# Blocks 4 to 11 in pairs: 512 tokens per up product, four down accumulators, six pooled PSUM banks, and an order written out

## The chip, the cores and the metric

The kernel runs on one core of a Trainium2 chip, in one launch. The metric is the device time of one execution in microseconds. The core's engines run at the same time and meet at semaphores: TensorE (PE) multiplies and writes to PSUM, VectorE (DVE) and ScalarE (ACT) read PSUM and compute element by element, GpSimd (POOL) computes element by element in SBUF, SyncE (SP) issues DMA.

## What is computed

A gated linear attention over 4 batches, 8 heads, 768 tokens and 40 values per head gives a state C and a normaliser n per head; its output y feeds a two-layer block. Everything is float32.

```python
for t in range(S):                       # attention, S = 768
    m_new = np.maximum(f_gate[:, :, t] + m, i_gate[:, :, t])
    f_stab = np.exp(f_gate[:, :, t] + m - m_new); i_stab = np.exp(i_gate[:, :, t] - m_new)
    C = f_stab * C + i_stab * (v_t outer k_t);  n = f_stab * n + i_stab * k_t
    y[:, :, t] = sigmoid(o_gate) * (C @ q_t) / max(|n . q_t|, 1)
x = y as (3072 tokens, 320)
h = x @ w_in                             # 320 -> 2048
sp = np.maximum(h, 0.0) + np.log1p(np.exp(-np.abs(h)))
out = (h * erf(sp)) @ w_out              # 2048 -> 320
```

The weights arrive as float64 and are decoded on the chip into a high and a low fp32r half (wh, wl for w_in; woh, wol for w_out).

## The kernel before

**Attention steps.** A chunk is 128 tokens; six chunks of four batches make 24 steps s. Step s loads q and k (`load`), k, v and the output gate (`loadv`), from chunk 1 on also rows of decays (`dq`) and of gate sums (`bq`, which reads cum_dr, written earlier by SP). POOL adds to the latter (`add`), ACT takes exp (`ex`), POOL masks it (`sel`). PE computes scores (`S`) and then outputs and new state (`ph`), DVE multiplies, adds and divides around them (`w`, `qa`, `sa`, `sk`, `yg`), ACT takes tanh of the gate (`th`), PE transposes the result (`tr`), and ACT and DVE split it into a high and a low half (`xh`, `xl`). From step 10 on, tr, S and ph of three neighbouring steps are one unit X on PE.

**Blocks and phases.** Two steps (256 tokens, T) make one of 12 blocks. A block passes through two phases, each with half of the 2048 hidden values, so there are 24 phases f. A phase has two groups of four 128-wide slices. In a group PE makes two up parts (`up`, L1023), each of two slices by eight products of 256 columns (high and low halves over three pieces of the 320 inputs) into one PSUM bank; `hb` copies each part out (DVE L1034 or ACT L1032); `sp` (L1046) and `er` (L1050) are softplus and erf on ACT, which loads a table at each switch; `mu` (DVE L1058) multiplies; `gh` (ACT L1064) and `gl` (DVE L1069) split it; then PE makes two down parts (`dn`, L1104, L1105, L1107), one for each of the block's two 128-token accumulators po0 and po1, each of 12 products of 320 columns. After the last group `o` (L1124) copies an accumulator out and `st` (L1131) stores it. Phases 0 and 1 use whole float32 weights (L1100). Until PE has work, it makes dummy products on a warm-up tile (`fill`, L445).

**Memory.** The eight PSUM banks are four for attention (`pa`), two for up parts (`h`), and po0 and po1. In SBUF a pool of 26 buffers of 4 KB per partition (`big`) holds loads, weights in work, and hb, e, gh, gl, xh and xl.

**Order.** A planner (class Plan) orders the parts by due times, costs per part, and tables of corrections, and issues them. On each engine the instructions run in that order, and an instruction at the head of its queue waits for its semaphores with all others of that engine behind it.

Of the kernel before, what the change touches and what calls it, by code (L numbers as in the profile page):

```python
# [9 lines left out]
F32 = mybir.dt.float32  # L10
# [19 lines left out]
NB = 2  # L30
# [10 lines left out]
class Buf:  # L41
    def __init__(self, tag):
        self.tag, self.users, self.left = tag, [], 0
        self.tags = ('big', tag) if tag in CAPS else (tag,)
# [6 lines left out]
class Plan:  # L51


    LAG = dict(PE=0.25, DVE=0.05, ACT=0.14, POOL=0.06, SP=0.0)
    RATE = 370.0
    AWAY, LANDING = 1.0, 1.2
    BEGIN = dict(SP=0.8, DVE=0.8, ACT=0.8, POOL=0.3, PE=0.8, dma=2.4)
    TABLE = 1.3
    FETCH = 5.8
    WINDOW, SINCE = 3.413, 1.3  # L60
    ENTER = {(3, 'D'): 0.1, (3, 'U'): 0.17, (1, 'D'): 0.22, (1, 'U'): 0.29, (2, 'D'): 0.22, (2, 'U'): 0.29, (1, 3): 0.12,
             (2, 3): 0.12, (1, 2): 0.1, (2, 1): 0.1, (3, 1): 0.09, (3, 2): 0.09, ('D', 1): 0.09, ('U', 1): 0.09,
             ('D', 2): 0.09, ('U', 2): 0.09}

    def __init__(self, slots):
        self.parts, self.slots, self.filler = [], dict(slots), None
        self.reset()

    def add(self, engine, cost, n=0, *, fn, after=(), new=(), use=(), target=None, kb=0.0, table=None, mode=0, order=(), lock=False):
        p = Part()  # L70
        p.engine, p.cost, p.fn, p.kb, p.table, p.mode, p.size = engine, cost, fn, kb, table, mode, n
        p.after = [x for x in after if x is not None]
        p.order = [x for x in order if x is not None]
        p.new, p.target, p.n = list(new), target, len(self.parts)
        for b in (*new, *use):
            b.users.append(p)
        p.held = [*new, *use]
        p.into, p.leaves, p.lock = None, mode, lock or engine == 'POOL'
        self.parts.append(p)
        return p  # L80

    def merge(self, name, members):
        p = self.add(members[0].engine, 0.0, fn=lambda: [m.fn() for m in members], mode=members[0].mode)
        p.name, p.leaves, p.size = name, members[-1].mode, sum(m.size for m in members)
        p.cost = sum(m.cost for m in members) + sum(self.ENTER.get((x.mode, y.mode), 0.0) for x, y in zip(members, members[1:]))
        p.after, p.order = ([x for m in members for x in getattr(m, of)] for of in ('after', 'order'))
        p.new = [b for m in members for b in m.new]
        p.held = list(dict.fromkeys(b for m in members for b in m.held))
        p.target = min((m.target for m in members if m.target is not None), default=None)
        for m in members:  # L90
            m.into = p
        for b in p.held:
            b.users = [x for x in b.users if x.into is not p] + [p]
        return p

    def tick(self, t, cost):

        while cost > 1e-9:
            k = max(0, int((t - self.SINCE) / self.WINDOW))
            while len(self.warm) <= k:  # L100
                busy = self.busy[len(self.warm) - 1] / self.WINDOW
                self.warm.append(busy > (0.65 if self.warm[-1] else 0.9))
                self.busy.append(0.0)
            pace = 1.0 if self.warm[k] else 2.0
            d = min(self.SINCE + (k + 1) * self.WINDOW - t + 1e-9, cost * pace)
            self.busy[k] += d
            t, cost = t + d, cost - d / pace
        return t

    def stream(self, t, cost, n):  # L110

        if not n:
            return self.tick(t, cost)
        each, end = cost / n, self.count + n
        while self.count < end:
            k = self.count // 256 + 1
            to = 256 * k - 48
            to = min(end, to if self.count < to else 256 * k)
            t, self.count = self.tick(t, (to - self.count) * each), to
            if to == 256 * k - 48:  # L120
                self.there[k + 1] = max(t, self.there.get(k, 0.0)) + self.FETCH
            elif to == 256 * k:
                t = max(t, self.there.get(k, 0.0))
        return t

    def reset(self):
        self.count, self.there, self.warm, self.busy = 68, {}, [True], [0.0]

    def lag(self, p):
        return self.AWAY + self.LANDING + p.kb / self.RATE if p.engine == 'SP' else self.LAG[p.engine]  # L130

    def issue(self):
        parts = self.parts = [p for p in self.parts if p.into is None]
        for i, p in enumerate(parts):
            p.n = i
            for of in ('after', 'order'):
                found = dict.fromkeys(x.into or x for x in getattr(p, of))
                found.pop(p, None)
                setattr(p, of, list(found))
# [1109 lines left out]
```

## Time and profile before

| | us |
|---|---|
| median of 3 runs | 476.99 (476.94 to 480.74) |
| span of the profiled execution | 474.6 |
| PE busy | 465.5 |
| PE weight loads busy | 433.4 |
| DVE busy | 336.2 |
| ACT busy | 330.7 |
| POOL busy | 117.9 |

The page counts an engine as busy while at least one instruction is in it. PE's products overlap, so the price of one in a stream is the distance between two starts, which the timeline shows. An engine's idle time costs nothing by itself; what matters is which wait ends last in a stage.

### The profile page before, as it was taken

The numbers are of one execution on the slowest core, as the hardware profiler recorded it, in microseconds if no ns is written. First come the engines' busy times: TensorE is split into PE (matmuls) and PEld (weight loads), VectorE is DVE, ScalarE is ACT, GpSimd is POOL, SyncE is SP. The second block draws the span as 40 slices with busy tenths as digits, with TensorE's granted clock in tenths as the row PEclk, the third lists the DMA queues.
The fourth block names the chain that finished last, engine by engine and source line by source line (L and its number), as shares of the span: only waits on it lengthen the run. The fifth ranks groups of instructions, "written<-read, shape, count | busy, mean of one in ns | idle before, by whom it ended". The sixth has DMA issues, their size and how long they took to land.

```text
span 474.6 us, 13831 instructions
## 1 busy us (share of the span) xinstructions
PE 465.5 (98%) x6091; PEld 433.4 (91%) x6095; DVE 336.2 (71%) x565; ACT 330.7 (70%) x385; POOL 117.9 (25%) x99
## 2 busy tenths in 40 slices
PE   9997999999999999999999999999999999999996
PEld 3567687999999999999999999999999999999996
DVE  4688799964688988897688498587487576466451
ACT  3574997499937998858655779458379556579670
POOL 2222147100912304043021454123453121010000
PEclk9998999999999999999999999999999999999999
DMA  7999525801174426045414405515313000000000
GB/s 260 381 298 308 141 93 177 301 1 55 47 227 134 106 88 185 1 152 161 136 43 135 135 17 155 143 35 156 122 35 120 19 17 15 1 17 13 1 28 28
DMA packets 28879, 53.25 MB, mean 112 GB/s; under 512 B 3060, under 2 KB 17844, under 8 KB 28820
## 3 DMA queue, kind: packets, MB, share of 16 engines
q1 hardware_dynamic: 28820, 52.38, 35.4%
q8 instruction: 47, 0.77, 0.7%
q14 instruction: 12, 0.10, 0.1%
HBM read 48.27 MB, written 4.10 MB: 110 GB/s over the span
## 4 chain that ended last, share of the span: by engine, by line
PE 88%; DMA 10%; SPq 1%; DVE 0%; POOL 0%; issue 0%; ACT 0%; POOLq 0%
PE h L1023 37%; PE po L1104 12%; PE po L1107 11%; PE po L1105 11%; PE pa L700 5%; DMA kvo<-in_kvo_dram 4%; PE po L1100 4%; PE pa L734 3%; DMA raw<-in_w_out_dram 3%; PE pa L738 3%; DMA raw<-in_w_in_dram 2%; PE pa L796 1%; PE pa L743 1%; DMA dq<-dec_dr 1%; PE po L445 0%; POOL wol L989 0%
## 5 line engine op out<-in xcount | busy, mean ns | idle before, releaser
L1023 PE MATMUL h<-xl,wh 128*128 128x256 f32 x576 | 158.1, 285 | 2.2 <-issue 1.9
L1023 PE MATMUL h<-xh,wh 128*128 128x256 f32 x576 | 158.7, 286 | 0.6 <-ACT xh L809 0.6
L1023 PEld LDWEIGHTS h<-xh,wh 128*128 128x128 f32 x576 | 111.1, 193 | 1.4 <-ACT xh L809 0.8
L1023 PEld LDWEIGHTS h<-xl,wh 128*128 128x128 f32 x576 | 111.1, 193 | 0.8 <-DVE xl L827 0.4
L1023 PE MATMUL h<-xh,wl 128*128 128x256 f32 x384 | 109.3, 285 | 0.8 <-issue 0.8
L1104 PE MATMUL po<-woh,gh 128*128 128x320 f32 x352 | 106.9, 316 | 0.0
L1105 PE MATMUL po<-wol,gh 128*128 128x320 f32 x352 | 104.6, 309 | 0.0
L1034 DVE COPY hb<-h 128x512 f32<-128x512 f32 x84 | 58.0, 690 | 62.8 <-PE h L1023 61.5
L1023 PEld LDWEIGHTS h<-xh,wl 128*128 128x128 f32 x384 | 74.1, 193 | 3.0 <-issue 3.0
L1046 ACT ACTIVATE e<-hb 128x1024 f32<-128x1024 f32 x48 | 50.3, 1057 | 26.1 <-DVE hb L1034 25.8
L1104 PEld LDWEIGHTS po<-woh,gh 128*128 128x128 f32 x352 | 66.2, 188 | 1.4 <-issue 0.2
L1105 PEld LDWEIGHTS po<-wol,gh 128*128 128x128 f32 x352 | 66.3, 188 | 0.0
L1107 PE MATMUL po<-woh,gl 128*128 128x320 f32 x352 | 66.2, 309 | 0.0
L1069 DVE TENSOR_TENSOR gl<-hb,gh 128x1024 fp32r<-128x1024 f32 x44 | 56.7, 1298 | 8.3 <-ACT gh L1064 7.9
L1058 DVE TENSOR_TENSOR hb<-e,hb 128x1024 f32<-128x1024 f32 x44 | 56.2, 1282 | 9.0 <-ACT e L1050 8.9
L1064 ACT ACTIVATE gh<-hb 128x1024 fp32r<-128x1024 f32 x44 | 45.6, 1050 | 24.1 <-DVE hb L1058 21.3
L784 POOL TENSOR_TENSOR kvo<-kvo,den 128x320 f32<-128x320 f32 x18 | 21.6, 1202 | 147.3 <-DVE kvo L778 78.8
L1107 PEld LDWEIGHTS po<-woh,gl 128*128 128x128 f32 x352 | 55.2, 188 | 0.2 <-issue 0.2
L1050 ACT ACTIVATE e<-e 128x1024 f32<-128x1024 f32 x48 | 49.0, 1053 | 0.3
L641 POOL TENSOR_TENSOR dm<-dm,aT 128x1024 f32<-128x1024 f32 x18 | 38.9, 2166 | 39.9 <-DVE aT L545 18.5
L716 DVE TENSOR_TENSOR dm<-pa,dm 128x512 f32<-128x512 f32 x48 | 30.9, 684 | 17.9 <-PE pa L700 15.9
L1046 ACT ACT_TABLE_LOAD x30 | 38.5, 1283 | 0.8 <-DVE hb L1034 0.3
(119 smaller groups left out, 636.9 us busy)
## 6 DMA issues: line engine op xcount, KB each, us to landing
kvo<-in_kvo_dram SPq DMA_DIRECT2D x24, 484.0 KB
dm<-cum_dr SPq DMA_DIRECT2D x18, 512.0 KB
qk<-in_qk_dram SPq DMA_DIRECT2D x12, 512.0 KB
qk<-in_qk_dram SPq DMA_DIRECT2D x12, 416.0 KB
raw<-in_w_in_dram SPq DMA_DIRECT2D x8, 512.0 KB
out_dram<-o SPq DMA_DIRECT2D x24, 160.0 KB
raw<-in_w_out_dram SPq DMA_DIRECT2D x8, 320.0 KB
dq<-dec_dr SPq DMA_DIRECT2D x20, 128.0 KB
```

Of the source, the lines that this page charges most:

```text
L641: nc.gpsimd.tensor_tensor(v.dm, v.dm, G.aT[:, b].unsqueeze(2).to_broadcast([128, H, L]), op=ALU.add)
L716: nc.vector.tensor_tensor(v.w[:, j], v.ps[j], v.w[:, j], op=ALU.mult)
L1023: nc.tensor.matmul(V.h[i][:, n % 2 * T:(n % 2 + 1) * T], w, m, start=(q == 0), stop=(q == len(ops) - 1))
L1034: nc.vector.tensor_copy(V.hb[:, i * 512:(i + 1) * 512], V.h[i])
L1046: nc.scalar.activation(V.e, V.hb, AF.Softplus)
L1050: nc.scalar.activation(V.e, V.e, AF.Erf)
L1058: nc.vector.tensor_tensor(V.g if full else V.hb, V.e, V.hb, op=ALU.mult)
L1064: nc.scalar.activation(V.gh, V.hb, AF.Copy)
L1069: (nc.gpsimd if f in GL_POOL else nc.vector).tensor_tensor(V.gl, V.hb, V.gh.bitcast(F32), op=ALU.subtract)
L1104: nc.tensor.matmul(K.po[b], V.gh[:, ts], woh[:, w], start=start, stop=False)
L1105: nc.tensor.matmul(K.po[b], V.gh[:, ts], wol[:, w], start=False, stop=False)
L1107: nc.tensor.matmul(K.po[b], V.gl[:, ts], woh[:, w], start=False, stop=stop)
```

## The change

Blocks 0 to 3 keep their phases. Blocks 4 to 11 are taken in four pairs: a pair has four phases of two groups, and a group has two 128-wide slices of 512 tokens instead of four of 256. An up part is then one slice of eight products of 512 columns, which fill one bank. A pair needs all four steps of its chunk before its first up part, and it has four accumulators, po0 to po3; a down part is two accumulators of six products of 320 columns. The four attention banks, the two up banks, po2 and po3 come from one pool of six (`bank`). xh and xl of a chunk are one wider buffer each, from a pool `xx` of four (6 KB per partition); `big` has 20 buffers. The planner is gone: a list of 1,292 parts, written out, gives the order, found by a search over orders.

```diff
-SLOTS = dict(pa=4, h=2, po0=1, po1=1, big=26, vg=2, dq=2, ...)
+SLOTS = dict(bank=6, po0=1, po1=1, big=20, xx=4, vg=2, dq=2, ...)
+BANKS = dict(pa=4, h=2, po2=1, po3=1)
...
-ORDER = [(k, hh) for hh in range(2) for k in range(EARLY)] + [(k, hh) for k in range(EARLY, NK) for hh in range(2)]
+PAIRED = 4
+ORDER = [((k,), hh) for hh in range(2) for k in range(EARLY)] + [((k,), hh) for k in range(EARLY, PAIRED) for hh in range(2)]
+ORDER += [((k, k + 1), q) for k in range(PAIRED, NK, 2) for q in range(4)]
+SEQUENCE = """
+ident small gload0 select minus fill cst win01 +1 zeros mask +1 load0 +1 tail0 +2 scan0 ones +1 loadv1 sum0 +1
...
     def new(pool, shape, dtype, tag):
-        return pool.tile(shape, dtype, name=tag, bufs=SLOTS[tag])
+        kind = 'bank' if tag in BANKS else tag
+        return pool.tile(shape, dtype, name=tag, tag=kind, bufs=SLOTS[kind])
...
+        nb = NB * len(ks)
+        width, nj = nb * L, W // (nb * L)
...
+                mine = range(nj * p + i * nj // 2, nj * p + (i + 1) * nj // 2)
...
-                            nc.tensor.matmul(V.h[i][:, n % 2 * T:(n % 2 + 1) * T], w, m,
+                            nc.tensor.matmul(V.h[i][:, n * width:(n + 1) * width], w, m,
                                              start=(q == 0), stop=(q == len(ops) - 1))
...
-                        K.po[b] = new(ps, [128, 512], F32, f"po{b}")[:, 0:DM]
+                        K.po[half] = [new(ps, [128, 512], F32, f"po{b}")[:, 0:DM] for b in of]
...
-    parts = plan.issue()
     with tc.manual_schedule():
-        for p in parts:
-            p.fn()
+        plan.issue(SEQUENCE)
```

On PE, half of an up part of blocks 4 and later before (one of its two slices; h is the bank, xh and xl the halves of x, wh and wl those of w_in):

```order
L1023 MATMUL h_3558<-xh_2985,wh_78 128x256
L1023 MATMUL h_3558<-xl_2986,wh_78 128x256
L1023 MATMUL h_3558<-xh_2985,wl_79 128x256
L1023 MATMUL h_3558<-xh_2985,wh_78 128x256
L1023 MATMUL h_3558<-xl_2986,wh_78 128x256
```

and the start of a whole one after (the two xx are the halves of x, of four steps):

```order
L840 MATMUL h_3870<-xx_3191,wh_78 128x512
L840 MATMUL h_3870<-xx_3192,wh_78 128x512
L840 MATMUL h_3870<-xx_3191,wl_79 128x512
L840 MATMUL h_3870<-xx_3191,wh_78 128x512
L840 MATMUL h_3870<-xx_3192,wh_78 128x512
```

A product has twice the columns, and a part has 8 products instead of 16.

On SP, the first loads of the program before (gt gates, raw float64 weights, qk and kvo the inputs of a step):

```order
L427 DMA cst<-in_consts_dram 128x12
L495 DMA gt<-in_gates_dram 128x2x128
L891 DMA raw<-in_w_in_dram 128x1024
L578 DMA qk<-in_qk_dram 128x1024 x2
L589 DMA kvo<-in_kvo_dram 128x968 x2
L906 DMA raw<-in_w_in_dram 64x1024 x2
L578 DMA qk<-in_qk_dram 128x1024
L891 DMA raw<-in_w_in_dram 128x1024 x2
L578 DMA qk<-in_qk_dram 128x1024
```

and after:

```order
L304 DMA gt<-in_gates_dram 128x2x128
L235 DMA cst<-in_consts_dram 128x12
L703 DMA raw<-in_w_in_dram 128x1024
L387 DMA qk<-in_qk_dram 128x1024
L718 DMA raw<-in_w_in_dram 64x1024 x2
L398 DMA kvo<-in_kvo_dram 128x968
L703 DMA raw<-in_w_in_dram 128x1024
L398 DMA kvo<-in_kvo_dram 128x968
L387 DMA qk<-in_qk_dram 128x1024 x2
```

The two qk, two kvo, and the raw pieces of the first block stand first; the qk of steps 2 and 3 and a further piece of w_in, which stood among them, come later (load1 is the first of the last x2).

On SP, the loads of steps 12 to 14 before (the qk in the middle of the first four rows is that of step 13):

```order
L1131 DMA out_dram<-o 128x320
L581 DMA qk<-in_qk_dram 104x1024
L1131 DMA out_dram<-o 128x320
L637 DMA dm<-cum_dr 128x1024
L589 DMA kvo<-in_kvo_dram 128x968
L581 DMA qk<-in_qk_dram 104x1024
```

and after (the first qk is that of step 13, dm that of step 14, the last two qk those of steps 14 and 15):

```order
L951 DMA out_dram<-o 128x320
L410 DMA dq<-dec_dr 64x4x128
L410 DMA dq<-dec_dr 40x4x128
L951 DMA out_dram<-o 128x320
L390 DMA qk<-in_qk_dram 104x1024
L446 DMA dm<-cum_dr 128x1024
L390 DMA qk<-in_qk_dram 104x1024 x2
```

X13 is the first part on PE that reads the qk of step 13. Before, 18 parts of PE (X11, X12, eight up and eight down parts) stand between that load and X13 in the order of parts; after, two down parts do.

## Rows read from the trace of the kernel before

**Rows 1.** From the page, part 1: engines, busy us (share), instructions.

```profile
PE 465.5 (98%) x6091; PEld 433.4 (91%) x6095; DVE 336.2 (71%) x565; ACT 330.7 (70%) x385; POOL 117.9 (25%) x99
```

**Rows 2.** From the page, the chain that ended last: its shares of the span by line.

```profile
PE h L1023 37%; PE po L1104 12%; PE po L1107 11%; PE po L1105 11%; PE pa L700 5%; DMA kvo<-in_kvo_dram 4%; PE po L1100 4%; PE pa L734 3%; DMA raw<-in_w_out_dram 3%; PE pa L738 3%; DMA raw<-in_w_in_dram 2%; PE pa L796 1%; PE pa L743 1%; DMA dq<-dec_dr 1%; PE po L445 0%; POOL wol L989 0%
```

**Rows 3.** Busy us by stage: length, PE, PEld, DVE, ACT, POOL, clock, DMA, GB/s.

```profile
0.00:34.47 34.47, 32.97 (x469) 17.74 (x472) 22.34 (x59) 18.39 (x34) 7.59 (x16) 1.00 0.91 313
34.47:87.58 53.11, 49.28 (x638) 40.27 (x637) 46.04 (x91) 39.00 (x61) 20.01 (x16) 0.97 0.61 189
87.58:470.80 383.22, 383.13 (x4990) 375.38 (x4988) 267.83 (x417) 272.88 (x289) 90.28 (x68) 1.00 0.28 84
470.80:474.60 3.80, 0.16 (x2) 0.00 (x0) 0.00 (x0) 0.44 (x1) 0.00 (x0) 0.91 0.18 63
```

**Rows 4.** PE timeline: start us, us, instruction; and line L445's durations, ns.

```profile
421.36 0.28 PE L1023 MATMUL h<-xh,wh 128*128 128x256 f32 x1
...
423.28 0.31 PE L1104 MATMUL po<-woh,gh 128*128 128x320 f32 x1
...
425.04 0.28 PE L1023 MATMUL h<-xh,wh 128*128 128x256 f32 x1
...
19.34 2.56 PE L445 MATMUL po<-warm 128*128 128x512 bf16 x11 [0.16 <-issue]
...
L445 PE MATMUL po<-warm x61: 378/379/634, 1.1 to 49.6; 128*128 128x512 bf16 x61
```

**Rows 5.** From the page, costliest groups: busy us, mean ns, idle before it.

```profile
L1034 DVE COPY hb<-h 128x512 f32<-128x512 f32 x84 | 58.0, 690 | 62.8 <-PE h L1023 61.5
L1046 ACT ACTIVATE e<-hb 128x1024 f32<-128x1024 f32 x48 | 50.3, 1057 | 26.1 <-DVE hb L1034 25.8
L1069 DVE TENSOR_TENSOR gl<-hb,gh 128x1024 fp32r<-128x1024 f32 x44 | 56.7, 1298 | 8.3 <-ACT gh L1064 7.9
L1058 DVE TENSOR_TENSOR hb<-e,hb 128x1024 f32<-128x1024 f32 x44 | 56.2, 1282 | 9.0 <-ACT e L1050 8.9
L1064 ACT ACTIVATE gh<-hb 128x1024 fp32r<-128x1024 f32 x44 | 45.6, 1050 | 24.1 <-DVE hb L1058 21.3 <-PE h L1023 2.7
L1050 ACT ACTIVATE e<-e 128x1024 f32<-128x1024 f32 x48 | 49.0, 1053 | 0.3
L1046 ACT ACT_TABLE_LOAD x30 | 38.5, 1283 | 0.8 <-DVE hb L1034 0.3
```

**Rows 6.** PE's waits: us in total, times, the longest us.

```profile
PE h L1023 <- issue: 2.7, 2, 1.9
```

**Rows 7.** PE timeline around the longest of them, and the window after it.

```profile
41.08 0.28 PE L1023 MATMUL h<-xh,wh 128*128 128x256 f32 x1
43.26 0.28 PE L1023 MATMUL h<-xl,wh 128*128 128x256 f32 x1 [1.90 <-issue]
...
45.00:48.00 3.00, 3.00 (x19) 3.00 (x18) 2.08 (x7) 2.40 (x4) 0.00 (x0) 0.62 0.68 167
```

**Rows 8.** SP's issues of one load and of three, and the last window with bytes.

```profile
119.16 0.33 SPq L637 DMA_DIRECT2D dm<-cum_dr  x1
...
122.00:123.00 1.00, 1.00 (x11) 1.00 (x10) 0.64 (x2) 1.00 (x3) 1.00 (x1) 1.00 0.09 33
...
263.53 0.35 SPq L637 DMA_DIRECT2D dm<-cum_dr  x1
...
265.11 0.35 SPq L581 DMA_DIRECT2D qk<-in_qk_dram  x1
...
271.00:272.00 1.00, 1.00 (x15) 0.83 (x15) 0.83 (x2) 1.00 (x2) 0.00 (x0) 1.00 0.07 25
```

**Rows 9.** ACT's waits from 90 to 470 us: total, times, longest.

```profile
ACT kvo L657 <- DMA kvo<-in_kvo_dram: 7.7, 3, 5.8
```

**Rows 10.** Timeline at the end: the last down products, and the last copy.

```profile
470.21 0.75 PE L1107 MATMUL po<-woh,gl 128*128 128x320 f32 x4
471.00 0.44 ACT L1124 ACTIVATE o<-po 128x320 f32<-128x320 f32 x1 [1.32 <-PE po L1107]
```

More of the change, by code (lines that the diff above doesn't have):

```diff
@@ L51, with __init__ @@
 class Plan:
[L54 to L67, printed above, removed]
+    def __init__(self):
+        self.parts, self.filler = [], None
     def add(self, engine, cost, n=0, *, fn, after=(), new=(), use=(), target=None, kb=0.0, table=None, mode=0, order=(), lock=False):
         p = Part()
[L71 to L78, printed above, removed]
+        p.fn, p.order, p.into = fn, [], None
         self.parts.append(p)
@@ L82, in merge @@
     def merge(self, name, members):
[L83 to L87, printed above, removed]
@@ L88, in merge @@
-        p.held = list(dict.fromkeys(b for m in members for b in m.held))
-        p.target = min((m.target for m in members if m.target is not None), default=None)
+        p = self.add('PE', 0.0, fn=lambda: [m.fn() for m in members])
+        p.name = name
         for m in members:
             m.into = p
-        for b in p.held:
-            b.users = [x for x in b.users if x.into is not p] + [p]
-        return p
[L96 to L124, printed above, removed]
@@ L267, with issue @@
-SLOTS = dict(pa=4, h=2, po0=1, po1=1, big=26, vg=2, dq=2, bits=2, den=2, gt=1, m_c=2, x0=2, aT=2, spl=1)
-CAPS = dict(qk=4, kvo=4, hb=4, e=3, gh=3, gl=3, raw=10, early=1, dm=3, xh=3, xl=3, o=4, w32=3, part=2, stk=4)
+        return p
+    def issue(self, sequence):
+        found = {}
+        for p in self.parts:
+            if p.into is None:
+                found.setdefault(p.name, []).append(p)
+        for token in sequence:
+            if token[0] == '+':
+                for _ in range(int(token[1:])):
+                    self.filler.fn()
+            else:
+                name, _, k = token.partition('.')
+                found[name][int(k or 0)].fn()
@@ L1041, in mlp @@
                 v.copies.append(copy)
-            @make(f'sp{f}', 'ACT', 0.97, after=copies, new=[e], use=[hb], table=('sp',))
+            @make(f'sp{f}', 'ACT', 1.0, after=copies, new=[e], use=[hb], table=('sp',))
             def sp(V=V):
@@ L1046, in sp @@
                 nc.scalar.activation(V.e, V.hb, AF.Softplus)
-            @make(f'er{f}', 'ACT', 0.97, after=[sp], use=[e], table=('er',))
+            @make(f'er{f}', 'ACT', 1.0, after=[sp], use=[e], table=('er',))
             def er(V=V):
@@ L1060, in mlp @@
             if not full:
-                @make(f'gh{f}', 'ACT', 0.97, after=[mu], new=[gh], use=[hb])
+                @make(f'gh{f}', 'ACT', 1.0, after=[mu], new=[gh], use=[hb])
                 def ghp(V=V):
```

429 lines of the change are left out of this document (165 added, 264 removed), and 71 rows, old and new, of tables (CHAIN, NUDGE).

## The prediction

> **What bounds the kernel now.** I read the page first. TensorE (PE) is busy 98% of the span [rows 1], and of the chain that ended last the up products (L1023) alone hold 37% of the span, the down products (po) 12 + 11 + 11 + 4 = 38%, and the four transfers named in it 4 + 3 + 2 + 1 = 10% [rows 2]. A share says nothing of where it holds, so I cut the span at three starts read from PE's timeline: 34.47 (first up product), 87.58 (first product of phase 2) and 470.80 (last product over). The table by stage shows four different things [rows 3]. Up to 34.47 the DMA engines are 0.91 busy: loads set the pace, and PE fills its waits with dummy products on a warm-up tile. From 34.47 to 87.58 weights are still arriving and being decoded, and PE is busy for 49.28 of 53.11 us, part of that at a lower clock. From 87.58 to 470.80 PE is busy 383.13 of 383.22 us at full clock, while DVE does 267.8 and ACT 272.9. Here nothing but PE's own work counts. The last 3.80 us are one copy out of PSUM and one store.
>
> In the third stage a product's price is its distance to the next one, not its busy time (products overlap). Sixteen up products of 256 columns go from 421.36 to 423.28, which is 0.120 us each, and twelve down products of 320 columns from 423.28 to 425.04, which is 0.147 each [rows 4]. The 64 extra columns cost 0.0267 us, or 0.417 ns a column (2.4 GHz), so both forms carry the same fixed 13.3 ns on top of their columns.
>
> **The change, part by part.** *Wide up products.* Blocks 4 to 11 need 1024 products of 256 columns before and 512 of 512 columns after. By the two rows a product of 512 costs 0.120 + 256 x 0.000417 = 0.2267 us, where it replaces 0.240. That is 13.3 ns x 512 = **6.8 us**, all on the path, since PE has no idle time in that stage. The trace has no fp32r product of 512 columns in a stream. The nearest rows bound it: the dummy bf16 products of 512 columns, eleven from 19.34 to 21.90, of which the last takes its own 0.38, so ten distances of 0.218 us [rows 4] (4.5 us more gain), and twice the narrow one, 0.240 (no gain). I take 0.2267, as the fixed part did not move between 256 and 320 columns. [...]
>
> *Down products.* The same 12 products of 320 columns per part, now for two accumulators: no change in number or price. Copies out of PSUM (hb, o) keep number and size.
>
> *Six pooled banks.* Before, an up product reused its bank after at least one other up part (1.92 us of PE work) against a copy of 0.69 us [rows 5]. Priced along the new order, the shortest distance to a reuse past the startup is 2.2 us, except in one place: the first up part of blocks 6 and 7 takes the bank of the third accumulator of blocks 4 and 5, seven distances of 0.147 (1.03 us) after the start of the last down product into it. At the end of the trace the last four down products start at 470.21, so the fourth at 470.65; its copy o starts at 471.00 and takes 0.44 [rows 10], so the bank is free 0.79 us after that start. 0.79 against 1.03: nothing, or 0.3 us if ACT is busy just then. I take 0.
>
> *The new order, startup.* The seven loads that the first up product needs are now the first seven large ones; before, three others stood among them. The order holds 56 dummy products instead of 65; nine at 0.218 are 2.0 us. The real work is the same. Two losses of 34.47 to 87.58 stand on PE: 2.7 us of waiting for "issue" in two up products [rows 6], the second of 1.9 at 43.26 with the DMA engines full, and after it a stretch at 0.62 of the clock [rows 7], which costs 0.38 x 3 = 1.1 us in 45 to 48 and some 0.3 before. What PE did before the fall was to stand from 41.2 to 43.26. In the new order SP holds at that time at the write of cum_dr, which waits for DVE, so the queue should be emptier; I take 2.6 of the 4.1 us back. Price of that hold: two w_out loads that the first down product needs stand behind it. One load lands about 4 us after its issue when alone [rows 8]; but two up parts (3.84 us) and the score and state products of steps 4 and 5 now stand ahead of that down product, where they stood behind it, so they hide it; without that cover it costs 4 us. Bounds for the startup: 6.1 gained, 4 lost. I take **4.6 gained**.
>
> *The new order, later.* In the third stage each down part must follow its last up part by the chain hb 0.69, table load 1.28, sp 1.06, table load 1.28, er 1.05, mu 1.28, gh 1.05, gl 1.30 [rows 5]: 9.0 us, plus queueing. PE work between the two, priced along the order, was 12.3 us at least before and is 11.5, 12.1 and 13.8 us at its tightest three places now. The chain still fits, with 2.5 us for queues. ACT loads a table 84 times instead of 79: 5 x 1.28 = 6.4 us on an engine with 110 us idle there; hidden unless it falls into one of those three places.
>
> What is tighter is loading. The pool of large buffers has 20 slots instead of 26 (four others hold the wider x). Along the order, counting PE work between the moment when slot and queue allow a load and its first reader, 20 of 69 loads after the startup have under 8 us and 8 have under 6; before it was 4 and 3 of 66. One load in the trace took about 4 us from issue (119.16) to the last byte; three issued within 1.6 us took 7.8 [rows 8]. So 8 loads can come up to 1.8 us late. Behind each on ACT (tanh of a gate) or POOL (an addition) wait that engine's later parts: sp, er and gh, for which PE's down parts wait. Before, ACT waited for such a load 3 times, 7.7 us in all [rows 9], and PE for none of it. Bounds: 0 (hidden again) and 20 x 1.8 = 36 (all passes). I take **2.0 us**, one load's lateness passing to PE. [...]
>
> **The sum**, against the profiled execution's 474.6: 474.6 - 6.8 - 2.0 - 2.6 + 2.0 = 465.2 us. The tail stays at 3.8: the last down part now has two accumulators, but the first is copied while PE works on the second. The median of the runs is 476.99, 2.4 over the span, so **467.6**.
>
> **The rivals.**
> 1. *Late loads reach PE.* If five of the eight tight loads pass their 1.8 us on, it is 9.0 instead of 2.0: 474.6, no change. For it: the counts above. Against it: mostly over 14 us between up and down parts.
> 2. *Slower, by the same queue.* All 20 loads with under 8 us pass something on. It decides at 0.8 us each: the kernel is slower by over 1% from 481.8, which is 16.2 us above the 465.6 without new waits, over 20 loads. At 1.2 us each it is 489.6. It needs PE to have less spare than the 2.5 us counted at the tightest place, at every place.
> 3. *The change does not do what it says:* the wide product costs 0.240, and its 6.8 us do not come: 474.4, no change. For it: only that no such product was seen; against it: the fixed 13.3 ns at two sizes.
> 4. *More comes:* a wide product at the dummy's 0.218: 463.1. For it: that row has 512 columns; against it: it is bf16.
>
> **How the numbers follow.** Forecast 0.68 (its own range 462 to 472, from the startup's 6.1 to 0 and waits of 0 to 4), late loads 0.13, slower 0.06, no gain in the product 0.05, a cheaper product 0.08. Forecast and the cheaper product are faster by over 1% (under 472.2): 0.76; rivals 1 and 3 are within 1%: 0.18; rival 2 is slower: 0.06. About 1% is what a measurement of this kernel tells from no change. The range 461.5 to 476 leaves out rival 2, and the ends of the others.
>
> **What would show it.** The wide up product starts 0.227 us apart; 0.218 or 0.240 would show rivals 4 or 3. Phase 2's first up product starts near 83 us; at 87 or later the startup term is wrong. From there to the last product it should be about 378 us, with PE idle under 3 us. PE waits for a load or a late gl in several places of over 1 us each, with ACT or POOL waiting for kvo or dm, would be rival 1 or 2. A clock under 1.00 after 50 us, or PE waiting for a bank, would be something that I have not priced.

## The result and the profile after

The changed kernel takes 472.31 us (median of four runs, 468.89 to 472.80) beside 478.3 for the kernel before in the same group: a ratio of 0.9869, 95% interval 0.9828 to 0.9911. Timed again later in ten runs beside the kernel before it was 472.9 us (470.26 to 476.92), ratio 0.9916 (0.9882 to 0.9951). It is faster by about 1%, 4 to 6 us, where 9.4 were forecast. Runs of different groups are compared by their ratio to the kernel before in the same group.

Part 1 of the page of after, to be read beside [rows 1]:

```profile
PE 457.5 (97%) x5569; PEld 404.0 (86%) x5574; DVE 335.0 (71%) x565; ACT 337.8 (72%) x390; POOL 105.1 (22%) x99
```

PE has 522 products fewer: 1024 became 512, and the rest are mostly dummies. The table by stage of after (columns as in [rows 3]), cut at the first up product, at the first product of phase 2 and at the end of the last product:

```profile
0.00:34.90 34.90, 31.13 (x457) 17.17 (x462) 23.22 (x60) 18.31 (x35) 7.50 (x17) 1.00 0.95 329
34.90:84.00 49.10, 48.22 (x641) 39.19 (x641) 46.05 (x91) 38.72 (x57) 15.78 (x14) 1.00 0.57 177
84.00:467.79 383.79, 378.18 (x4475) 347.65 (x4473) 265.75 (x416) 280.36 (x299) 81.83 (x69) 1.00 0.28 85
467.79:471.09 3.30, 0.00 (x1) 0.00 (x0) 0.00 (x0) 0.44 (x1) 0.00 (x0) 0.91 0.28 99
```

The whole gain of the profiled execution (474.6 to 471.1) lies ahead of phase 2, which starts 3.6 us earlier, and in the tail. The third stage, in which 512 products fewer should have saved 6.8 us, takes 383.8 us where it took 383.2. PE is no longer busy all through it: 5.6 us are idle. The view of PE's waits (us in total, times, the longest) says what for:

```profile
PE po L922 <- issue: 3.7, 1, 3.7
PE h L840 <- issue: 2.0, 1, 2.0
```

"issue" means that the engine waited for nothing that the profile shows. Before, the two waits of that kind (0.8 and 1.9 us) stood in the startup [rows 6]; now they stand in the stage where PE alone sets the time. The second profile of this kernel has both at the same products, 2.0 and 4.2 us long. PE's timeline around them (start, us, instruction, and in brackets the idle time before it):

```profile
135.20 0.28 PE L840 MATMUL h<-xx,wl 128*128 128x256 f32 x1
137.43 0.61 PE L840 MATMUL h<-xx,wh 128*128 128x256 f32 x4 [1.95 <-issue]
...
188.66 0.31 PE L921 MATMUL po<-woh,gh 128*128 128x320 f32 x1
192.62 0.42 PE L922 MATMUL po<-wol,gh 128*128 128x320 f32 x1 [3.66 <-issue]
```

Each stops in the middle of a part, between two products that wait for no other engine. Behind the second, TensorE's granted clock falls, as the busy time of three stretches shows (columns as above):

```profile
187.00:188.50 1.50, 1.50 (x77) 1.44 (x66) 1.50 (x2) 1.12 (x2) 0.35 (x1) 1.00 1.16 217
188.70:192.60 3.90, 0.26 (x2) 0.00 (x0) 1.96 (x6) 0.79 (x2) 1.83 (x3) 1.00 0.89 319
192.60:198.00 5.40, 5.38 (x23) 5.04 (x24) 1.86 (x4) 0.47 (x1) 0.00 (x0) 0.68 0.93 222
```

PE stood, and ran 3.4 of the next 5.4 us at a granted clock of 0.50 (0.50 all through from 194 to 197 us), as in before's startup [rows 7], where it is 0.50 from 44 to 46 us. The price of a product shows in a wide up part, eight products of 512 columns from 413.88 to 415.74:

```profile
413.88 0.62 PE L840 MATMUL h<-xx,wh 128*128 128x512 f32 x2
...
415.74 0.31 PE L921 MATMUL po<-woh,gh 128*128 128x320 f32 x1
```

1.86 us over eight is 0.2325 a product; over all wide products of the trace the mean distance is 0.2330. The forecast was 0.2267.

### The profile page after: what moved, and what is told of

The parts are those of the page before. It is cut to its first block, busy times and chain, and to the rows that moved or that the text cites. A ratio compares the mean times of both kernels' runs of the same rounds, so it can differ in the third digit from the quotient of the medians.

```text
span 471.1 us, 12874 instructions
## 1 busy us (share of the span) xinstructions
PE 457.5 (97%) x5569; PEld 404.0 (86%) x5574; DVE 335.0 (71%) x565; ACT 337.8 (72%) x390; POOL 105.1 (22%) x99
## 4 chain that ended last, share of the span: by engine, by line
PE 85%; DMA 8%; issue 2%; DVE 2%; SPq 2%; ACT 1%; DVEq 0%; ACTq 0%
PE h L840 35%; PE po L921 12%; PE po L924 11%; PE po L922 11%; PE pa L509 4%; PE po L917 4%; DMA raw<-in_w_out_dram 3%; PE pa L543 3%; PE pa L547 2%; DMA raw<-in_w_in_dram 2%; DMA qk<-in_qk_dram 2%; PE pa L605 1%; DMA kvo<-in_kvo_dram 1%; PE pa L552 1%; DVE bits L787 1%
## 5 line engine op out<-in xcount | busy, mean ns | idle before, releaser
L840 PE MATMUL h<-xx,wh 128*128 128x256 f32 (+1 forms) x768 | 177.4, 339 | 2.6 <-issue 2.0
L840 PEld LDWEIGHTS h<-xx,wh 128*128 128x128 f32 x768 | 126.8, 189 | 18.8 <-issue 2.0
L922 PE MATMUL po<-wol,gh 128*128 128x320 f32 x352 | 106.1, 310 | 3.7 <-issue 3.7
L840 PE MATMUL h<-xx,wl 128*128 128x256 f32 (+1 forms) x256 | 86.5, 338 | 0.0
L924 PE MATMUL po<-woh,gl 128*128 128x320 f32 x352 | 76.9, 311 | 0.0
L924 PEld LDWEIGHTS po<-woh,gl 128*128 128x128 f32 x352 | 58.3, 189 | 0.1
L840 PEld LDWEIGHTS h<-xx,wl 128*128 128x128 f32 x256 | 48.4, 189 | 5.7
L450 POOL TENSOR_TENSOR dm<-dm,aT 128x1024 f32<-128x1024 f32 x18 | 37.7, 2094 | 43.6 <-DVE dm L525 23.5
L593 POOL TENSOR_TENSOR kvo<-kvo,den 128x320 f32<-128x320 f32 x18 | 16.6, 920 | 108.3 <-DVE kvo L587 56.6
L459 POOL TENSOR_SCALAR_AFFINE_SELECT dm<-dm 128x1024 f32<-128x1024 f32 x18 | 21.9, 1220 | 67.6 <-ACT dm L454 66.5
```

The source lines that it names most:

```text
L450: nc.gpsimd.tensor_tensor(v.dm, v.dm, G.aT[:, b].unsqueeze(2).to_broadcast([128, H, L]), op=ALU.add)
L840: nc.tensor.matmul(V.h[i][:, n * width:(n + 1) * width], w, m, start=(q == 0), stop=(q == len(ops) - 1))
L922: nc.tensor.matmul(po, V.gh[:, ts], wol[:, w], start=False, stop=False)
L924: nc.tensor.matmul(po, V.gl[:, ts], woh[:, w], start=False, stop=stop)
```

## What the two waits are: PE's own program arriving

The page counts the transfers of instructions apart from the data. Part 3 of after has

```profile
q8 instruction: 44, 0.72, 0.7%
```

(packets, MB, share of the DMA engines): 44 packets of 16 KB. PE has 11,216 records in the trace (11,143 products and weight loads, and 73 of its sequencer), 255 for each packet. If a packet holds 256 instructions, the 44 are PE's program, fetched while it runs. The first wait comes behind 3,772 of these records, the second behind 5,564. They are 1,792 apart, and 7 x 256 is 1,792. So both waits stand at ends of blocks, seven blocks from each other. In the trace's list of packets, the one seven packets ahead starts at 134.98 and lands at 135.98, and PE goes on at 137.43; the other starts at 190.13, lands at 191.20, and PE goes on at 192.62. Both times PE resumes 1.4 us after the landing. Before's two startup waits fit too: packets landed at 34.89 and 41.93, PE resumed at 36.15 and 43.26. The fit holds well beyond these four. From 35 us on, the traces of both kernels and of all the runs below have 28 waits for "issue" of over 0.3 us, and every one stands behind a number of PE's records that leaves 188 to 190 when divided by 256, with PE going on 1.3 to 1.65 us after a packet's landing.

What the DMA engines did while PE stood the second time, from 188.7 to 190.1 and from 190.1 to 191.2 us (packets, MB, share):

```profile
q1 hardware_dynamic: 161, 0.47, 98.7%
...
q1 hardware_dynamic: 100, 0.35, 79.2%
q8 instruction: 1, 0.02, 6.1%
```

For 1.4 us data fill them and no packet of PE's program starts; it starts in the second window. The data come from SP's timeline:

```profile
177.68 0.39 SPq L390 DMA_DIRECT2D qk<-in_qk_dram  x1
178.16 0.34 SPq L446 DMA_DIRECT2D dm<-cum_dr  x1
178.60 0.76 SPq L390 DMA_DIRECT2D qk<-in_qk_dram  x2
179.45 1.39 SPq L410 DMA_DIRECT2D dq<-dec_dr  x2
180.93 1.86 SPq L398 DMA_DIRECT2D kvo<-in_kvo_dram  x2
183.03 0.33 SPq L446 DMA_DIRECT2D dm<-cum_dr  x1
```

Nine transfers, some 3.4 MB, are issued within 5.7 us: the queue of SP rows that the order showed, with the qk of steps 13, 14 and 15 side by side. And the block that ends at 188.66 began at 186.16: it holds the end of X12, whose products start some 10 ns apart, so 256 instructions were used up in 2.5 us. The block ahead of the first wait ran from 132.20 to 135.20. The last column but one is the share of the DMA engines, which were full during both:

```profile
132.20:135.20 3.00, 3.00 (x142) 2.93 (x133) 2.83 (x6) 2.97 (x4) 0.38 (x1) 1.00 1.01 407
186.16:188.66 2.50, 2.50 (x135) 2.44 (x135) 2.47 (x3) 1.28 (x3) 1.33 (x2) 1.00 1.09 213
```

In a stretch of wide up and down parts a block lasts 22 us (338.0 to 360.1). **Theory F**, formed from this: a block that is used up in about 3 us while the DMA engines are full makes PE wait for the next. (In before's startup blocks that lasted 5.0 and 4.9 us came late too, at a DMA share of 0.93 and 1.04, so 3 us is no bound.) Its rivals: **G**, X12 is simply too fast for any fetch, whatever the load; **H**, the wait belongs to the place in the program, to some semaphore that the profile doesn't show.

## Experiments

**Loads moved out of the burst.** The loads of q and k of steps 14 and 15 go behind the write of the decays:

```diff
-... xl10 dn6.3 load14 load15 qa12 mu7.0 X13 ... dn7.1 xl11 y12 load16 th13
+... xl10 dn6.3 qa12 mu7.0 X13 ... dn7.1 xl11 y12 load14 load15 load16 th13
```

> The kernel after, with the loads of q and k of steps 14 and 15 moved behind the write of the decays (decw4), out of a burst of eight loads that is issued from 177.7 to 183.0 us. Theory F (the 3.7 us wait at 188.66 is a 16 KB block of PE's instructions that comes late because the DMA engines are full of that burst, after X12 used up a block in 2.5 us): 0.83 of 3.4 MB less lies ahead of the block, at some 300 GB/s 2.7 us, so the wait shrinks from 3.7 to about 1 us or nothing, the stretch of half clock behind it goes too, and the time falls by 3 to 5 us against after's runs of 472. Rival G (X12 uses up its instructions faster than they can be fetched, whatever the load): the wait stays near 3.7 us. The wait of 2.0 us at 135.2 us stays in both.

PE's waits in it:

```profile
PE h L840 <- issue: 2.2, 1, 2.2
PE pa L349 <- DVE x L327: 2.2, 1, 2.2
```

and its DMA packets from 186 to 189.4 us (packets, MB, share):

```profile
q1 hardware_dynamic: 263, 0.91, 66.6%
q8 instruction: 1, 0.02, 2.0%
```

The wait behind X12 is all but gone. At the same product (189.44) the distance to the next is 0.45 us where it was 3.96, and the packet lands at 188.54, before PE is through with the block. That block too was used up in 2.5 us (186.90 to 189.44), but at a DMA share of 0.55 instead of 1.09. The other wait, at 134 us, stayed, as nothing was moved there. For the wait behind X12 that is F and not G; for the other no run changed the load. The time did not follow: 472.4 us against 472.9 for after, ratio 0.9916 for both, no difference. A new wait of 2.2 us at 216 us has taken its place: PE's transpose of gate sums (`at5`, L349) waits for `rest5` on DVE; in after PE comes there later and finds it done. And the clock falls around both waits, where in after it fell around one:

```profile
136.00:140.00 4.00, 3.30 (x16) 3.29 (x16) 1.61 (x6) 3.96 (x4) 1.50 (x1) 0.57 0.42 116
218.00:222.00 4.00, 3.38 (x14) 3.42 (x15) 3.97 (x8) 3.23 (x5) 1.89 (x1) 0.57 0.26 86
```

Each of the two costs 0.43 x 4 = 1.7 us.

**Blocks moved along the program, first try.** The 56 dummy products become 28 plain float32 ones, which were expected to take twice as long each, to have 56 instructions fewer ahead of all else:

```diff
-        nc.tensor.matmul(early.bank, warm, warm[:, 0:1].to_broadcast([128, 512]), start=True, stop=True)
+        early.n += 1
+        if early.n % 2:
+            nc.tensor.matmul(early.bank, ident, m0.to_broadcast([128, 512]), start=True, stop=True)
```

> The kernel after, with its 56 dummy bf16 products replaced by 28 plain float32 ones, which take about twice as long each: the same PE time, 28 products (56 instructions) fewer ahead of everything else. The blocks of 256 instructions in which PE's program is fetched then begin 56 instructions later in the program. Theory F (late block): the two blocks that came late at 135.20 and 188.66 us are needed 28 products later, some 3.3 and 4 us, and both waits shrink to under 1 us or go; no other block is used up in under 2.9 us while the DMA engines are full, so the time falls by 4 to 7 us to 465 to 468. Rival H (the wait belongs to the place in the program, to X12 and what follows it, or to a semaphore): both waits stay at 2.0 and 3.7 us. If dummy products matter otherwise (the clock at the start), the first up product moves from 34.9 us.

It missed its aim. A plain float32 product is recorded as two (5,571 products in all, where after has 5,569), so no block moved, and with 0.43 us between the starts of the two halves it takes as long as four dummies (0.218 us each), not two: the first up product came at 42.9 us instead of 34.9, and the time is 483.0. Both waits stayed in their places in the program (2.0 and 3.8 us). F and H say the same of that.

**Blocks moved, second try.** A hundred tiny products behind the twentieth dummy:

```diff
+        early.n += 1
+        for _ in range(100 * (early.n == 20)):
+            nc.tensor.matmul(early.bank[0:32, 0:32], warm[:, 0:32], warm[:, 0:32], start=True, stop=True)
```

> The kernel after with 100 tiny products (32 x 32 columns) behind its twentieth dummy product, some 8 us into the program, where PE waits for loads. They add 200 instructions, so that each block of 256 instructions begins 200 earlier in the program, which is 56 later than the block after it. (The attempt to do the same with halved dummy products left the number of instructions as it was, since a plain float32 product of 512 columns is recorded as two.) Theory F (a block that is used up in under some 3 us while the DMA engines are full makes PE wait for the next): worked out on the trace of after, the blocks that ended at 135.20 and 188.66 us now end 28 products later, where 3.3 and 4 us more have passed; both waits go or fall under 1 us, with them the half clock behind the second (1.2 us), and the time falls by 4 to 7 us, to 465 to 468. Rival H (the waits belong to their places in the program): both stay at 2.0 and 3.7 us, time as after.

PE's waits of over 1 us behind the startup in it:

```profile
PE pa L352 <- DVE x L330: 2.1, 1, 2.1
```

Both waits for instructions are gone, with the same loads, the same products and the same order around them: H falls, F holds. The two packets came no earlier: they start 2.7 and 3.9 us after the block ahead of them began (in after 2.8 and 4.0), and the DMA engines are as full in that time:

```profile
132.89:135.54 2.65, 2.65 (x117) 2.58 (x106) 2.53 (x5) 2.62 (x4) 0.05 (x1) 1.00 1.03 415
184.78:188.70 3.92, 3.92 (x127) 3.86 (x116) 3.00 (x7) 1.67 (x4) 2.65 (x4) 1.00 1.00 302
```

But the blocks ahead of them now last 5.5 and 7.1 us instead of 3.0 and 2.5, so PE does not need them yet. The time gains again less than expected: 471.9 us, ratio 0.9889 (0.9837 to 0.9940), expected 465 to 468; the runs don't tell it from after. The third stage is shorter (380.62 us from phase 2 to the last product, after 383.79), but PE stands at `at5` for 2.1 us as in the run with the loads moved, and then goes at the lower clock:

```profile
217.00:220.00 3.00, 3.00 (x10) 2.54 (x10) 2.45 (x2) 2.94 (x3) 1.37 (x1) 0.50 0.00 0
```

and the tiny products set the first up product back to 35.5 us (33.9 to 34.9 in the traces whose startup is that of after).

**That, with `at5` behind a down part.**

```diff
-... rest5 qa14 at5 at4 o7.0 dn8.1 hb9.2 ...
+... rest5 qa14 o7.0 dn8.1 at5 at4 hb9.2 ...
```

> The kernel with 100 tiny products, and the two transposes of gate sums (at5, at4) behind one down part on PE instead of ahead of it. With the tiny products alone both waits for instructions were gone, but PE then stood 2.1 us at at5 (212.8 us), for DVE's rest5, which was no earlier than in after, and after it ran at half clock from 217 to 220 us. If that wait is what gave part of the gain back, the down part covers it (1.76 us), the half clock goes, and the last product ends 2 to 3 us earlier than the 464.98 of the kernel with tiny products alone: span 465 to 466. If DVE is behind in all of that stretch, the wait moves on to the next part that needs DVE and the span stays at 468.

The last product ends at 463.56 (464.98 with the tiny products alone), and its largest waits behind the startup are small:

```profile
PE pa L555 <- issue: 0.9, 1, 0.9
PE h L843 <- DVE hb L854: 0.8, 1, 0.8
```

The down part took the wait's place, and the clock stays at 1.00; some 1.4 us came of the 2 to 3 expected. The time is 470.7, ratio 0.9861 (0.9826 to 0.9895), the span 466.9. (The 0.9 us at L555 are again the end of a block, at another place.)

**The price of a product by itself.** Behind the last product of after, 12 accumulating products at each of 32 starts of the moving operand, for three widths, and the same with the weights moved instead (left out here); then a finer table:

```diff
+        for width in (512, 256, 320):
+            for o in range(32):
+                for q in range(12):
+                    nc.tensor.matmul(table[:, 0:width], wl[:, 0, q * 128:(q + 1) * 128], flat[:, o * 32:o * 32 + width], start=q == 0, stop=q == 11)
```

> The kernel after, with products added behind its last one that nobody reads: 12 accumulating fp32r products each of 512, 256 and 320 columns, for 32 starts of the moving operand 128 bytes apart (in woh), then the same with the start of the weights moved instead. Nothing else runs then, so distances are prices. Theory A (the fixed part of a product depends on where its moving operand starts): the price of 256 columns moves between about 113 and 120 ns with the start, that of 512 between about 220 and 233, and moving the weights changes nothing. Theory B (the fixed part grows with the columns, whatever the place): one price per width at all starts, near 233 ns for 512. Theory C (the prices differ because of the other engines at work in the kernel): one price per width here, and lower than 113 or 230 ns.

> As the price table, with the start of the moving operand in steps of 16 bytes over 256 bytes, and some starts repeated. In the first table 512 columns cost 227 ns at starts of 128 and 233 ns at starts of 0 modulo 256 bytes, at all 32 places, and 256 and 320 columns hardly moved (118.5 to 119 and 146.5). In the kernel after, whose x starts at 64 modulo 256, 512 columns cost 233.0. Theory A (the start modulo 256 bytes sets the price): 233 at 64 too, and one price at each start however often it is repeated. Theory D (the phase in which a stream of products starts sets the price, as the 113.5 and 118.0 ns of the narrow products suggest, which change from stream to stream at one and the same start): starts at 64 modulo 128 give two prices in the repetitions.

Distances of starts in ns (means over a stream of twelve without its first distance; the first table has 16 places of each kind; ranges over places or repetitions; the starts are those of the buffers' addresses in the program, where woh begins at 128):

| start modulo 256 bytes | 512 columns | 256 columns | 320 columns |
|---|---|---|---|
| 0, first table | 232.8 to 232.9 | 118.6 to 118.7 | 146.6 to 146.7 |
| 128, first table | 227.6 to 228.7 | 118.2 to 118.7 | 145.6 to 146.6 |
| 0, fine | 231.6 to 233.1 | 117.7 to 118.7 | 146.1 to 148.3 |
| 64, fine | 232.9 | 114.5 to 117.8 | 146.7 to 147 |
| 128, fine | 226.6 to 229.8 | 119.2 to 119.5 | 146.7 |
| 192, fine | 228.9 to 229.8 | 113.3 to 118.0 | 146.7 to 147 |

With nothing else at work, 512 columns cost some 233 or some 228 ns, by where x starts; other starts in steps of 16 bytes lie between 226.7 and 234.7. For 512 columns that is theory A in its main point. Its last part fell: with x at 128 and the weights moved instead, 512 columns cost 228.9 to 229.8 ns for weights at 128 and 232.1 to 232.2 for weights at 0, so the start of both counts. Columns alone (B) would give one price, and other engines (C) are not there. With 320 columns two starts stand out, 80 and 208, with 152 and 153 ns. With 256 columns A does not hold: one and the same start gives two prices (D holds there). In after, streams of narrow products run at 113 to 114 or at 118 ns, and the products from the start of phase 2 on at 118 in after and at 113 in the run with the loads moved, with the same instructions ahead of them. What decides it stays open.

**The wide products undone, in the order of after.**

```diff
-                        for q, (w, m) in enumerate(ops):
-                            nc.tensor.matmul(V.h[i][:, n * width:(n + 1) * width], w, m, ...)
+                        for c in range(0, width, T):
+                            for q, (w, m) in enumerate(ops):
+                                nc.tensor.matmul(V.h[i][:, n * width + c:n * width + c + T], w, m[:, c:c + T], ...)
```

> The kernel after, in which a wide up part makes its 512 columns as two passes of eight products of 256 columns (16 products, as before); order, buffers and copies are those of after. The prediction's term (each product carries the same 13.3 ns) expects 512 x 13.3 ns = 6.8 us more than after. The trace of after has the wide product at 233.0 ns and the narrow one at 118.0 (first half of a chunk's x) and 113.5 (second half): by the theory that the place of the moving operand sets the price a part goes from 8 x 233.0 = 1864 ns to 8 x (118.0 + 113.5) = 1852 ns, so 64 parts change the time by -0.8 us, no difference. The wait for instructions at X12 (3.7 us near 188 us) should be there again in most executions, since the instructions ahead of it are the same.

An up part of 16 narrow products in it, from 418.18 to 420.00:

```profile
418.18 0.40 PE L841 MATMUL h<-xx,wh 128*128 128x256 f32 x2
...
420.00 0.31 PE L922 MATMUL po<-woh,gh 128*128 128x320 f32 x1
```

1.82 us, where the wide part took 1.86. The narrow products of this layout cost 115.3 ns in the mean of the trace; so with x at this place the wide product by itself saves nothing. Yet the time is 475.5 us (ratio to before 0.9973, interval 0.9944 to 1.0001), some 3 us over after, where no difference was expected. The waits show where:

```profile
PE po L922 <- issue: 3.9, 2, 3.6
PE po L923 <- issue: 3.9, 2, 3.6
PE h L841 <- issue: 1.6, 1, 1.6
```

There is a third large wait, at 278.8 us, with a granted clock of 0.57 in the mean from 283 to 287 us behind it: 1,024 instructions more move the ends of the blocks, and one of them now falls behind another attention unit. What the wide product brings in this order is half the instructions of the up parts, and by that other ends of blocks. Fewer instructions alone do not spare the waits: before has as many records as this run (12,222 and 12,240) and no such wait behind its startup.

**x moved by 64 bytes.** The moving operands of wide products start at 128 modulo 256 bytes instead of 64 (those of narrow ones stay):

```diff
-                R.xh, R.xl = (new(sb, [128, 3, B * L], F32R, "xx") for _ in range(2))
+                o = [(0, 48, 32, 16), (16, 0, 48, 32)][s // B >= PAIRED // 2][s // B % 2 * 2:]
+                R.xh, R.xl = (new(sb, [128, 1584], F32R, "xx")[:, a:a + 3 * B * L].rearrange("p (n t) -> p n t", n=3) for a in o[:2])
```

> The kernel after, with x of blocks 4 to 11 placed 64 bytes further in its buffers, so that the moving operand of each wide product starts at 128 modulo 256 bytes instead of 64; the x of blocks 0 to 3 stays at 64, and nothing else moves. By the two price tables a wide product then costs 226.6 to 229.8 ns instead of 232.9: 512 of them take 1.6 to 3.2 us less, and the rows of the trace show it directly. If the price in the kernel has another cause (other engines at work, as rival), it stays at 233. The waits for instructions stay as in after, so the time is 469 to 472, against 472.9 for after in the group before.

A wide part in it, from 413.61 to 415.44, 1.83 us:

```profile
413.61 0.63 PE L841 MATMUL h<-xx,wh 128*128 128x512 f32 x2
...
415.44 0.30 PE L922 MATMUL po<-woh,gh 128*128 128x320 f32 x1
```

The mean of all is 227.9 ns, where it was 233.0: 512 x 5.1 = 2.6 us, as the tables say. The time is 471.2 us, ratio 0.9878 (0.9837 to 0.9919): as expected, and by itself not to be told from after, whose own times differ by as much. The price is shown by the trace.

**Both together.** The tiny products, `at5` moved and x moved.

> Both: the kernel of tiny_at with x of blocks 4 to 11 at 128 modulo 256 bytes. If the two gains add (2 to 3 us from the start of the operand, 4 to 7 us from the waits for instructions), the time is 464 to 467 against 472.9 of after and 476.9 of before: faster than both by more than 1%.

467.6 us (464.96 to 468.77), ratio to before 0.9795, interval 0.9764 to 0.9826, which lies wholly below those of after (0.9828 to 0.9911 and 0.9882 to 0.9951). That is a little over the 464 to 467 expected; the first up product comes at 36.24 us, and one end of a block costs 1.2 us at 265 us. Its third stage:

```profile
85.73:462.89 377.16, 374.71 (x4475) 346.11 (x4473) 265.64 (x416) 280.41 (x299) 83.94 (x69) 1.00 0.28 87
```

377.2 us, 2.4 less than with the tiny products and `at5` alone (463.56 - 83.99 = 379.6) and 6.6 less than in after: the two gains add. This is the version to keep, and the only one that its times show to be faster than after.

**The startup, from after.** The write of cum_dr on SP moves behind four loads:

```diff
-... hb0.1 deco3 cumw1 th5 tr2 ... loadv4 hio3 xl2 yy3 decw1 ...
+... hb0.1 deco3 th5 tr2 ... loadv4 hio3 xl2 yy3 cumw1 decw1 ...
```

> The kernel after, with the write of cum_dr of chunk 1 (cumw1) moved on SP behind four loads (two of w_out, one of gates, one of k, v and o) that stood behind it. In after SP waits there from 32.2 to 40.4 us, the DMA engines are 0.11, 0.01 and 0.07 busy from 36 to 42 us, and PE's instruction blocks land 2.0 us ahead of need at 41.5. If that quiet is what took the two waits and the half clock of before's startup away (1.1 + 1.9 + 1.4 us), then loads issued into it bring part of them back: the first product of phase 2 moves from 84.0 to 85 to 87 us, with a wait for instructions near 36 or 42 us. If the startup gain comes from the order of the first loads alone, phase 2 starts at 84.0 as before, or earlier, since the four loads come earlier.

Its time is 475.6 us, ratio 0.9955 (0.9921 to 0.9990), 2.6 us over the 472.9 of after in the same group; the two intervals still overlap. Phase 2 starts at 86.47 us, 2.5 to 3.5 later, as the first theory said, but not by its mechanism: no large wait for instructions stands in the startup. The w_out loads were through by 39 us, before the next block was needed, and cum_dr was written 3.6 us later (43.99 instead of 40.38). DVE waits for that write, what it does behind comes later (L327 at 55.57 us instead of 54.16 in after), PE's transpose of gate sums waits for that, and the clock falls behind (one line each of DVE's timeline, PE's waits and the busy time):

```profile
48.27 0.49 DVE L363 SCALAR_TENSOR_TENSOR x<-spl,cst,x 128x256 f32<-128x256 bf16 x1 [1.16 <-DMA cum_dr<-x]
PE pa L349 <- DVE x L327: 1.4, 1, 1.4
58.00:62.50 4.50, 4.50 (x26) 3.80 (x23) 4.46 (x6) 2.27 (x5) 3.66 (x3) 0.62 0.53 149
```

PE's wait is 1.4 us and the clock costs 0.38 x 4.5 = 1.7 us, enough for the 2.5 us. So the run doesn't tell whether the quiet helps; it shows that the hold on SP stands where it does for cum_dr's sake.

**The startup, from before.** The tiny products (108) in the kernel before.

> The kernel before, with 108 tiny products behind its twentieth dummy product: each block of 256 instructions begins 216 earlier in the program, 40 later than the block after it. In the trace of before PE waits for instructions at 35.04 and 41.08 us (1.1 and 2.2 us between starts), and a stretch at half clock follows (1.4 us); blocks there were used up in 5.0 us and would take 6.1 and 6.5 now. If the startup's gain of 3.6 us in after is these waits, before without them gains 2 to 4 us of it: phase 2 starts at 84 to 86 instead of 87.6 us and the time is 473 to 475. If the startup's gain is the order of the first loads, phase 2 stays at 87 to 88 and the time at 477.

Its time is 476.6 us, ratio 1.000 (0.997 to 1.003). From the first up product to phase 2 it takes 50.77 us instead of 53.11, at full clock:

```profile
36.47:87.24 50.77, 47.52 (x638) 38.73 (x637) 46.01 (x92) 39.21 (x61) 19.97 (x16) 1.00 0.57 175
```

One of the two startup waits is gone and with it the lower clock; the other (2.2 us) now stands at 44.4. But the tiny products set the first up product back from 34.47 to 36.47, which takes the gain. The stretch of lower clock in before, by its mean over six microseconds:

```profile
43.00:49.00 6.00, 5.69 (x33) 5.49 (x34) 4.05 (x9) 3.40 (x5) 1.25 (x1) 0.72 0.71 165
```

That is 0.28 x 6 = 1.7 us of clock, and the waits fell from 2.7 to 2.2 us: together 2.2 of the 2.3 us. It speaks for waits and clock as the cause of the 4.0 us by which after is faster between the two points, as it has neither. It doesn't settle it, since the later start gives the loads 2 us more as well.

## Why the prediction was right and wrong

The sign and the range held. The likeliest time was 467.6 and the measured 472.3: the gain was about half of what was forecast, and the terms differ more than the sum. That the time fell into the range is in part luck: what took the gain away, waits for instructions and the clock behind them, stood in none of the rivals and in no bound of the range, and a cheaper narrow product, which was not priced, gave some of it back. The profiled execution of after against that of before, in us:

| term | forecast | measured |
|---|---|---|
| 512 wide products | -6.8 | -3.6 (512 x (240 - 233) ns) |
| narrow products from phase 2 on (blocks 0 to 3) | 0 | -1.5 (384 x (119.8 - 115.8) ns) |
| up to the first up product (nine dummies fewer) | -2.0 | +0.4 |
| from there to phase 2 | -2.6 | -4.0 |
| late loads | +2.0 | 0 |
| waits for instructions in the third stage, by starts of products | 0 | +5.9 |
| the lower clock behind them (5.40 us at 0.68) | 0 | +1.7 |
| tail | 0 | -0.5 |
| sum | -9.4 | -1.6; the trace has -3.5 |

Of the 1.9 us between the last two numbers some 1 us are three products of the decoding of weights, which the new order makes ahead of phase 2; the rest was not traced.

*Wide product.* The step that failed is "I take 0.2267, as the fixed part did not move between 256 and 320 columns". It does move: on top of its columns (512 x 0.417 = 213 ns) the wide product carries 233 - 213 = 20 ns with x at its place in after, and 228 - 213 = 15 with x 64 bytes further. The term was mis-sized by 3.2 us: 3.6 came of 6.8, between the forecast and rival 3 (0.240); rival 4's 0.218 was seen nowhere. The bounds around the value held it. The narrow product's price wasn't fixed either, which no row of before could show, as all of before's x start at 128. The place of x decides what the width is worth. At 128, where before has x, a wide product (227.9 in the run with x moved) against two narrow ones (2 x 119.8) saves 11.7 ns, or 6.0 us for 512, close to the forecast (8 to 12 ns by the tables, 4 to 6 us). The change put x at 64, and there two narrow ones cost 230.6 (2 x 115.3) and a wide one 233.0: the width saves nothing, and the 3.6 us came with the place.

*Startup.* Dummy products fill a wait; taking nine away does not end it. DMA is 0.95 busy up to 34.90, and the first up product came at 33.9 to 34.9 in the traces that have this startup, where before has 34.47. The other term was right in kind: the two "issue" waits [rows 6] and the half clock [rows 7] (0.50) went, and the DMA share from 36 to 42 us is 0.11, 0.01 and 0.07 (in before 1.02, 1.04 and 1.10). The half clock had cost 1.7 us and not the 1.4 that the prediction read. That the quiet is why was read off the trace and not shown by a run.

*Late loads.* The count was right and its consequence was not. ACT and POOL (from 84 to 470 us) wait for loads more often than before [rows 9]:

```profile
ACT kvo L466 <- DMA kvo<-in_kvo_dram: 22.9, 7, 7.1
...
POOL dm L450 <- DMA dm<-cum_dr: 14.1, 7, 5.6
```

37.0 us in all, against 19.2 before (ACT 7.7 in three waits, POOL 11.5 in one), and PE waits for none of it. The spare between up and down parts held it, so rivals 1 and 2 did not come. But the same crowding came through another door. The prediction had "PE waiting for 'issue'" with full DMA engines in its rows, named it as a loss of the startup, and took it as gone with a quieter queue; it did not ask where else the DMA engines would be full while PE uses up its program fast. That term, waits for instructions in the third stage, stood at nothing without a reason, and measured 5.9 us and 1.7 us of clock. The SP rows with four transfers of steps 13 to 15 side by side were in front of it.

*Where the expected gain went.* Into two waits of the engine that sets the time, each behind a block used up while the DMA engines were full, and into a product that is 6 ns dearer than thought. Removing the waits gives back only part at first, since PE then arrives early at a transpose for which DVE is not ready (2.1 to 2.2 us in two runs); moved behind a down part, that is gone too.

## What to carry to other kernels

When PE runs at 100% of a stage, count its instructions too, and look where it uses up 256 of them in a few microseconds (streams of short products; here 2.5 to 5.0 us in after and before): no burst of loads should stand there (with the DMA share at 0.55 instead of 1.09, the 3.96 us behind X12's block became 0.45), and instructions added far ahead (200 here) can move the block's end to a place where it costs nothing. Price a new operand shape in a table of its own behind the last product, at the operand addresses that the kernel will use, before counting on a constant taken from two other shapes: here 64 bytes decided whether the wide product was worth 4 to 6 us or nothing. And taking away filler work that only fills a wait gained nothing here: with nine dummies fewer the first up product came at 33.9 to 34.9 us, where before has 34.47.

## What the runs showed of the hardware

- TensorE's program of this kernel comes in blocks of 256 instructions; a late block cost up to 4.3 us (in the run with the write of cum_dr moved), with PE resuming 1.3 to 1.65 us after the block's packet landed. In before and in after the granted clock fell to 0.50 for 3.4 us behind the longer of two such waits (1.9 and 3.7 us), and stayed at 1.00 behind the shorter (0.8 and 2.0).
- A stream of fp32r products of 512 columns costs 227 to 230 ns each where the moving operand starts at 128 modulo 256 bytes, and 232 to 233 at 0 and 64.
- One of 256 columns costs 113 to 114 or 118 ns with x at 64, where it changes from stream to stream, and 118 to 120 with x at 128.
- A plain float32 product of 512 columns stands in the trace as two, with 0.43 us between their starts.
